# SyncE in written order in the projections, with later stores of the features and recall's loads one place ahead

## The chip, the cores and the metric

The kernel runs on one core of one Trainium2 chip. The metric is the device time of one execution in microseconds (us). TensorE is called PE, VectorE DVE, ScalarE ACT, GpSimd POOL, and SyncE SP; SP issues every DMA of this kernel.

## The reference

```python
x = A_x                                                    # [1, 2048, 576]
g = sigmoid((x * gate_w).sum(-1, keepdims=True))
# A: 32 heads of 18, N = 4 segments of L = 512 tokens, with a memory M, z that runs over the segments
phi = lambda t: where(t > 0, t + 1.0, exp(t))
for s in range(4):
    qs, ks, vs = q[:, :, s], k[:, :, s], v[:, :, s]
    a_dot = softmax(qs @ ks.T * 18 ** -0.5 + causal mask) @ vs
    a_mem = (phi(qs) @ M) / (phi(qs) @ z + 1e-6)
    outs.append(sigmoid(beta) * a_mem + (1 - sigmoid(beta)) * a_dot)
    M, z = M + phi(ks).T @ vs, z + phi(ks).sum()
a = concat(outs) @ wo
b = (gelu(x @ w_gate) * (x @ w_up)) @ w_down               # 576 -> 4608 -> 576
out = g * a + (1 - g) * b
```

## The kernel before, in words

All large products are made in pairs of float16 words (high and low), three matmuls for one. The kernel has two parts. The first, up to about 241 us, makes the projections q, k, v of the four segments, the memory and the recall from it. The second is a loop of 72 steps, with the feed-forward part and the attention interleaved, and then the output projection.

The first part goes over the segments s = 0 to 3. A segment s has *rows* (for s > 0): four groups q of 128 tokens, in which `vrows` makes v in two halves (q, 0) and (q, 1), `key_rows` transposes phi(k) of the segment before, and `memorize` adds to the memory's product. Then come its *columns*: nine chains j = 0 to 8 of 14 matmuls each (`project`), 128 columns of q and k at a time. What a chain leaves in PSUM is read in the next column (`put_columns`): ACT takes the high word, an exponential for phi follows on ACT, DVE makes phi and the low word (`rest`, `words`), POOL adds the exponential, and two DMAs store the words to `qk`. `rest` is put off into a list (`later`) that `finish_later` works off a little later in the same column.

For s >= 1 phi(q) of a segment is kept as float32 and split later by `split_phi` (ACT high, POOL low, two stores to the DRAM tile `phq`). In segment s + 1, `load_phi(s, g)` loads the features of eight heads (two DMAs, 256 KB each, into the single buffer `phg`), `recall(s, g)` multiplies them with the memory (16 small matmuls into two banks, "st" or "dn"), and `put_recall` divides on DVE and stores to `om`. The four groups g = 0 to 3 follow each other. In the last segment's case (s = 3) they run in the first steps of the loop.

The memory's own chain runs in the columns of the next segment: `keep_memory` at j = 1, `memory_squares` at j = 2, `memory_scales` at j = 4 (a sum on PE, a root on DVE, six small operations on POOL), `memory_pairs` at j = 6 (two ACT copies, a POOL subtraction, two stores to `md`, two loads into `mpair`, which recall multiplies with).

`load_x16` loads a segment of x (three DMAs, 1280 KB) and `load_sums` two segments once more (two DMAs of 1024 KB each). `load_g` loads a block of w_gate and w_up (640 KB); ACT squares it, and the sums of the squares (`scales(0)`, in the rows of s = 3 at q = 1) stand in PE's order.

PE, ACT, DVE and POOL run in the order in which the code is written (`manual_schedule(engines=ORDERED)`). SP is not in that set before the change: the scheduler chooses the order of the DMAs. The PSUM tags are "dn" and "st" with two banks each, and "pv", "V", "G", "U" with one.

Of the kernel before, what the change touches and what calls it, by code (L numbers as in the profile page):

```python
# [18 lines left out]
P = 128  # L19
# [26 lines left out]
def kernel(ctx: ExitStack, tc: tile.TileContext, xs, wqk, wv, wo, wgu, wd, beta, out):  # L46
# [8 lines left out]
    def bank(tag, bufs=1, dt=F32):  # L55
        return ps.tile([P, 512 if dt == F32 else 1024], dt, name=tag, tag=tag, bufs=bufs)
# [20 lines left out]
    def root(out, inv, src):  # L77

        dve.tensor_scalar(out.bitcast(I32), src.bitcast(I32), 1, EXP, OP.logical_shift_right, OP.bitwise_and)
        dve.tensor_scalar(inv.bitcast(I32), out.bitcast(I32), EXP, None, OP.bitwise_xor)  # L80
# [12 lines left out]
    def sums(st, o=None):  # L93

        o = (spare() if o is None else o)[:, : st.shape[1]]
        pe.matmul(o, onesb, st.bitcast(BF16)[:, 1::2], start=True, stop=True)
        return o
# [461 lines left out]
    if True:  # L559
# [15 lines left out]
        xt = [mp.tile([P, 15, L], F16, name="xt0", bufs=1)]  # L575
        kept.update(words=flat(acc), xt=xt)
        pa = first.enter_context(tc.tile_pool(name="early", bufs=2, reuse_waits="tile"))
        W, phi, vst, kr, mem, phis, phg, ghs = {}, {}, {}, {}, {}, [], {}, {}
        QG = ((0,), (1,), (2,), (3,), (4, 5), (6, 7), (8,))
        VG = ((0,), (1,), (2,), (3,), (4,))  # L580
        VB = (slice(0, NH), slice(NH, D + 2))
# [78 lines left out]
        def split_phi(until):  # L660
            while phis and phis[0][:2] <= until:
                s, j, f = phis.pop(0)
                m = min(P, D - j * P)
                st = pp.tile([P, 2, L], F16, name="stage", bufs=5)
                act.activation(st[:m, 0], f[:m], AF.Copy)
                pool.tensor_tensor(st[:m, 1], f[:m], st[:m, 0], OP.subtract)
                r = phq[s - 1][j * P : j * P + m]
                sp.dma_start(r[:, :2], st[:m])
                sp.dma_start(r[:, 2], st[:m, 0])

        def load_phi(s, g):
            r = phq[s - 1].rearrange("f a t -> (f a) t")
# [5 lines left out]

        def put_columns(s, j, pr):
            hf, c = divmod(s, 2)  # L680
            st = pp.tile([P, 2, L], F16, name="stage", bufs=5)
            unit = unq if j < 4 else 2.0**-14
            i = 2 if j < 4 else 0
# [144 lines left out]
                act.activation(m16[:, :, 2, c], mc[:, :, c], AF.Square, accum_out=q[:, i : i + 1])  # L828
            return q

        def memory_scales(s, q):
            o = sums(q, bank("dn", 2))
            v = pp.tile([P, 2, 2], F32, name="mv", bufs=1)
            z = pp.tile([P, 2], F32, name="mz", bufs=1)
            dve.tensor_scalar(z, o, 1e-30, None, OP.max)
            root(v[:, 0], v[:, 1], z)
            u = pp.tile([P, 2], F32, name="mu", bufs=1)
            pool.tensor_scalar(u, v[:, 1], 2.0**-50, None, OP.mult)
            g, eps = ghs[s + 1] = pp.tile([P, H], F32, name="ghs", bufs=2), pp.tile([P, 1], F32, name="eps", bufs=2)
            for i, c in enumerate((slice(0, DH), slice(DH, MC))):  # L840
                pool.tensor_scalar(mt[:, :, c], mc[:, :, c], u[:, i : i + 1], None, OP.mult)
            pool.tensor_scalar(g, gh[:, 0], u[:, 1:2], v[:, 0, 0:1], OP.mult, OP.mult)
            pool.tensor_scalar(g, g, 2.0**49, None, OP.mult)
            pool.tensor_scalar(eps, u[:, 1:2], kmc[:, s + 1, 1:2], 1e-6, OP.mult, OP.mult)

        def memory_pairs():
            act.activation(m16[:, :, 0], mt, AF.Copy)
            act.activation(m16[:, :, 1], m16[:, :, 0], AF.Copy)
            pool.tensor_tensor(m16[:, :, 2], mt, m16[:, :, 0], OP.subtract)
            sp.dma_start(md[: 4 * MT].rearrange("(j p) a c -> p j a c", p=MT), m16[:MT, :4])  # L850
            sp.dma_start(md[4 * MT :], m16[: D - 4 * MT, 4])
            n = 3 * DH
            r = md.rearrange("(i e f) a c -> e (f a) i c", e=2, f=DH)
            for e in range(2):
                sp.dma_start(mpair[64 * e : 64 * e + n, :, e * MC : (e + 1) * MC], r[e])
# [19 lines left out]
            dve.tensor_scalar(gate[:, 1, gs], gate[:, 0, gs], -1.0, 1.0, OP.mult, OP.add)  # L875

        FIRST = (0,)
        with tc.manual_schedule(engines=ORDERED):
            pool.memset(onesb, 1.0)

            start = bank("G")
# [214 lines left out]
            for s in range(4):  # L1096
                p = s - 1
                if s:
                    for q in range(4):
# [15 lines left out]
                        pv = vrows(s, q, 1)  # L1115
                        put_rows(s, q, 1, *pv)
                        if p >= 1:
                            if q < 2:
                                split_phi((p, 2 if q == 0 else 4))
                            else:  # L1120
                                recall(p, q - 2)
                            if q:
                                load_phi(p, q - 1)
                        if q:
                            memorize(p, q - 1)
                    finish_later()
# [1 line left out]
                for j in range(9):  # L1128
# [39 lines left out]
                    if s and j == 2:  # L1168
                        square = memory_squares()
                    if s and j == 4:  # L1170
                        memory_scales(p, square)
                    if s > 1 and j in (3, 5):
                        recall(p, (j + 1) // 2, "dn")
                        if j == 3:
                            load_phi(p, 3)
                    if s and j == 6:
                        memory_pairs()
                    if s == 3 and j == 8:
                        load_phi(3, 0)
            put_columns(*done)  # L1180
            finish_later()
            split_phi((3, 4))
            ahead[0] = first_product(0)
            finish_later()

# [801 lines left out]
```

## Time and profile before

| what | value |
|---|---|
| median of 3 runs | 1591.38 us (1590.36 to 1592.06) |
| profiled execution | 1592.69 us, its span 1591.0 us |
| PE busy | 1550.5 us, 97% of the span |
| DVE, ACT, POOL busy | 1265.6, 1217.6, 1161.4 us |
| PE idle in 100.79 to 241.40 us | 32.1 us of 140.6 |
| granted clock of PE over the span | 0.99 |

The span is the time from the first to the last instruction of the profiled execution; the device time holds 1.7 us more. Lines as L758 are lines of the kernel before. A bracket behind a row of the timeline says how long the engine was idle before it and what ended that. The last row but one counts PE's idle time from the rows of s = 2 to the end of the first part.

### The profile page before, as it was taken

What the parts mean: (1) busy time and instruction counts of PE and PEld (TensorE: products, weight loads), DVE (VectorE), ACT (ScalarE), POOL (GpSimd) and SP (SyncE); (2) the same over time, 40 slices, a digit from 0 to 9 for tenths busy, and PEclk for the clock granted to TensorE, in tenths of its full rate; (3) what the DMA queues carried; (4) which work ended last, traced back from release to release, by engine and by line L of the source; (5) the groups of instructions that cost most, each with busy time, mean ns of one, the idle gap of its engine ahead of it and who ended that gap; (6) DMA issues with size and microseconds to landing.
All of it is one profiled execution on the core that took longest, in us unless ns stands there. A gap on an engine that the chain in (4) does not pass through costs nothing.

```text
span 1591.0 us, 33969 instructions
## 1 busy us (share of the span) xinstructions
PE 1550.5 (97%) x12271; PEld 944.8 (59%) x12271; DVE 1265.6 (80%) x3249; ACT 1217.6 (77%) x2092; POOL 1161.4 (73%) x1260
## 2 busy tenths in 40 slices
PE   9988689999999999999999999999999999999999
PEld 5644444556666665656666556656566666656577
DVE  7867577688888888888888888888888888888665
ACT  7575363588888878888888888888888888887421
POOL 4284485687868687787868696777878686877597
PEclk9999799999999999999999999999999999999999
DMA  6655757246566675656575766567575766755546
GB/s 242 231 170 150 206 169 186 61 111 143 132 149 139 125 146 123 128 125 145 126 156 131 144 141 134 134 121 149 117 151 132 154 136 131 150 117 101 116 83 174
DMA packets 513156, 225.83 MB, mean 142 GB/s; under 512 B 435768, under 2 KB 491804, under 8 KB 512476
## 3 DMA queue, kind: packets, MB, share of 16 engines
q1 hardware_dynamic: 512988, 223.67, 61.2%
q8 instruction: 96, 1.57, 0.4%
q14 instruction: 72, 0.59, 0.1%
HBM read 97.47 MB, written 37.52 MB: 85 GB/s over the span
## 4 chain that ended last, share of the span: by engine, by line
PE 83%; POOL 7%; DVE 3%; ACT 3%; DMA 2%; issue 1%; SPq 0%; POOLq 0%; ACTq 0%; DVEq 0%
PE dn L1337 25%; PE U L535 17%; PE G L535 11%; PE V L535 6%; PE V L1457 5%; PE pv L1290 4%; PE U L1383 2%; PE V L1388 1%; PE G L1388 1%; PE st L1252 1%; PE st L414 1%; PE dn L421 1%; PE V L1383 1%; PE G L1383 1%; PE dn L1252 1%
## 5 line engine op out<-in xcount | busy, mean ns | idle before, releaser
L535 PEld LDWEIGHTS <-pairg 128*128 128x128 f16 x2592 | 247.9, 98 | 263.6 <-issue 17.6
L1273 POOL TENSOR_TENSOR pl<-pb,ph 128x896 f16<-128x896 f32 (+1 forms) x128 | 185.7, 1472 | 211.3 <-ACT ph L1272 211.3
L1337 PE MATMUL dn<-paird,hhr 128*128 128x288 f16 x2115 | 328.7, 286 | 0.1
L1271 ACT ACTIVATE pb<-pb,mb,esc 128x512 f32<-128x512 f32 (+3 forms) x512 | 304.9, 642 | 5.2
L1345 DVE SCALAR_TENSOR_TENSOR acc<-dn,ev,acc 128x288 f32<-128x288 f32 x533 | 262.6, 513 | 39.3 <-PE dn L1337 33.3
L1337 PEld LDWEIGHTS <-hhr 128*128 128x128 f16 x2160 | 207.0, 98 | 78.6 <-issue 11.8
L535 PE MATMUL G<-x,pairg 128*128 128x512 f16 x864 | 210.4, 380 | 5.5 <-DVE stage L703 4.5
L535 PE MATMUL U<-xt,pairg 128*128 128x512 f16 x864 | 209.9, 379 | 0.0
L1337 PE MATMUL dn<-paird,hhd 128*128 128x288 f16 x1275 | 209.8, 286 | 0.0
L1273 POOL TENSOR_TENSOR pb<-pb,ph 128x896 f16<-128x896 f32 (+1 forms) x128 | 179.4, 1402 | 33.3 <-ACT ph L1272 27.7
L1272 ACT ACTIVATE ph<-pb 128x896 f16<-128x896 f32 (+1 forms) x256 | 188.6, 737 | 9.7
L347 POOL TENSOR_TENSOR pairg<-raw,pairg 128x384 f16<-128x384 f32 (+2 forms) x144 | 157.5, 1115 | 20.2 <-ACT pairg L343 20.2
L1255 DVE CUSTOM_DVE_ANT_0 pb<-st,mask 128x512 f32<-128x512 f32 (+1 forms) x256 | 157.2, 614 | 0.0
L1337 PEld LDWEIGHTS <-hhd 128*128 128x128 f16 x1296 | 123.9, 98 | 50.4 <-issue 6.5
L1255 DVE CUSTOM_DVE_ANT_0 pb<-dn,mask 128x256 f32<-128x256 f32 (+1 forms) x192 | 67.2, 375 | 64.2 <-PE dn L1252 62.5
L1457 PE MATMUL V<-xt,nest 128*128 128x256 f16 x714 | 105.5, 272 | 0.0
L535 PE MATMUL V<-x,pairg 128*128 128x512 f16 x426 | 105.1, 383 | 0.1
L535 PE MATMUL U<-x,pairg 128*128 128x512 f16 x432 | 105.0, 379 | 0.2 <-DVE gl L1653 0.2
L1378 ACT ACTIVATE gl<-gl,sc 128x512 f32<-128x512 f32 x110 | 75.8, 715 | 34.0 <-DVE gl L1653 23.0
L1375 POOL TENSOR_TENSOR hhr<-gl,hhr 128x512 f16<-128x512 f32 x64 | 78.9, 1239 | 14.6 <-ACT hhr L1367 14.5
L1290 PEld LDWEIGHTS <-pt 128*128 128x128 f16 x2560 | 80.8, 96 | 13.1 <-issue 8.4
L343 ACT ACTIVATE pairg<-raw 128x384 f16<-128x384 f32 (+2 forms) x144 | 77.8, 587 | 10.1 <-DVE raw L309 6.1
(371 smaller groups left out, 3197.7 us busy)
## 6 DMA issues: line engine op xcount, KB each, us to landing
qkt<-qk SPq DMA_DIRECT2D x256, 108.0 KB
raw<-in_wgu_dram SPq DMA_DIRECT2D x36, 640.0 KB
rawd<-in_wd_dram SPq DMA_DIRECT2D x36, 288.0 KB
qk<-stage SPq DMA_DIRECT2D x32, 256.0 KB
phg<-phq SPq DMA_DIRECT2D x24, 256.0 KB
qk<-stage SPq DMA_DIRECT2D x40, 128.0 KB
vp<-vstage SPq DMA_DIRECT2D x16, 296.0 KB
vt<-vp SPq DMA_DIRECT2D x16, 296.0 KB
```

Source lines behind the costliest of these rows:

```text
L343: act.activation(spot(f, *p, 0), raw_g[f][:, p[0] : p[1]], AF.Copy)
L347: pool.tensor_tensor(spot(f, *p, 1), raw_g[f][:, p[0] : p[1]], spot(f, *p, 0), OP.subtract)
L535: pe.matmul(o, w[:, i, (a + k) * P : (a + k + 1) * P], x[:, b + k], start=start and k == 0 and i == 0 and b == h, stop=k == 1 and i == 1, ...
L1255: dve.tensor_tensor_reduce(scored(a, qi), out[qi], mask[:, L - (qi + 1) * P :], 1.0, -3e38, OP.add, OP.max, mx[a][:, qi : qi + 1])
L1271: act.activation(r, r, AF.Exp, bias=b[:, qi : qi + 1], scale=esc[:, 0, c : c + 1])
L1272: act.activation(h[:, cols], p, AF.Copy)
L1273: pool.tensor_tensor(low[:, cols], p, h[:, cols], OP.subtract)
L1290: pe.matmul(ov, pr[:, 10 * i + COL[qi] // P + kb], v[:, 4 * e + kb, c0 : c0 + VC], start=kb == 0 and i == 0, stop=kb == qi and i == 1)
L1337: pe.matmul(o[:, :NH], hh[:, a, q * P : (q + 1) * P], w[:, b, n * NH : (n + 1) * NH], start=i == 0, stop=i == 5)
L1345: dve.scalar_tensor_tensor(av, o[:, :NH], ev, av, OP.mult, OP.add)
L1375: pool.tensor_tensor(hh[:, 1], t, hh[:, 0], OP.subtract)
L1457: pe.matmul(o, w[:, (7 * c + i) * P : (7 * c + i + 1) * P], x[d], start=start and n == 0, stop=n == 2, skip_group_check=True)
```

## The change

SP joins the engines that keep the written order, in the first part only. `split_phi` no longer issues its two stores but keeps them in a list; `store_phi` issues them at the next place (the next `put_columns`, or the next group of rows). `recall(p, 0)` goes from the rows' q = 2 to q = 3, recall 1 from q = 3 to behind column 1; recalls 2 and 3 stay behind columns 3 and 5. Each load of recall in the columns stands one column ahead of its recall, behind columns 0, 2 and 4. The sum of `memory_scales` becomes `memory_root`, in the bank "pv" and at j = 4; the rest of it follows at j = 5; `memory_pairs` is cut into `memory_high` (j = 6), `memory_low` (j = 7) and `load_pairs` (j = 8).

```diff
         def split_phi(until):
 ...
-                r = phq[s - 1][j * P : j * P + m]
-                sp.dma_start(r[:, :2], st[:m])
-                sp.dma_start(r[:, 2], st[:m, 0])
+                phi_out.append((phq[s - 1][j * P : j * P + m], st[:m]))
+
+        def store_phi():
+            while phi_out:
+                r, st = phi_out.pop(0)
+                sp.dma_start(r[:, :2], st)
+                sp.dma_start(r[:, 2], st[:, 0])
 
         def put_columns(s, j, pr):
             hf, c = divmod(s, 2)
+            store_phi()
 ...
-        def memory_scales(s, q):
-            o = sums(q, bank("dn", 2))
+        def memory_root(q):
+            o = sums(q, bank("pv"))
 ...
             root(v[:, 0], v[:, 1], z)
+            return v
+
+        def memory_scales(s, v):
 ...
-        def memory_pairs():
+        def memory_high():
             act.activation(m16[:, :, 0], mt, AF.Copy)
             act.activation(m16[:, :, 1], m16[:, :, 0], AF.Copy)
+
+        def memory_low():
             pool.tensor_tensor(m16[:, :, 2], mt, m16[:, :, 0], OP.subtract)
 ...
+        def load_pairs():
 ...
-        with tc.manual_schedule(engines=ORDERED):
+        with tc.manual_schedule(engines=ORDERED | {mybir.EngineType.SP}):
 ...
                         if p >= 1:
+                            if q:
+                                store_phi()
                             if q < 2:
                                 split_phi((p, 2 if q == 0 else 4))
-                            else:
-                                recall(p, q - 2)
-                            if q:
-                                load_phi(p, q - 1)
+                            if q == 2:
+                                load_phi(p, 0)
+                            if q == 3:
+                                recall(p, 0)
 ...
                     if s and j == 4:
-                        memory_scales(p, square)
-                    if s > 1 and j in (3, 5):
-                        recall(p, (j + 1) // 2, "dn")
-                        if j == 3:
-                            load_phi(p, 3)
+                        mv = memory_root(square)
+                    if s and j == 5:
+                        memory_scales(p, mv)
+                    if s > 1 and j < 6:
+                        if j % 2:
+                            recall(p, (j + 1) // 2, "dn")
+                        else:
+                            load_phi(p, j // 2 + 1)
                     if s and j == 6:
-                        memory_pairs()
+                        memory_high()
+                    if s and j == 7:
+                        memory_low()
+                    if s and j == 8:
+                        load_pairs()
 ...
             split_phi((3, 4))
+            store_phi()
```

Three places show how SP's order moves. The first is SP in the columns of s = 2, around the load of recall 3 (`phg_1829` before, `phg_1890` after). `stage_1794` and `stage_1844` hold the words of columns 2 and 3 in their order of before and after, and `mo` is what a put_recall leaves. Before:

```order
L709 DMA qk_74<-stage_1724 128x512
L709 DMA qk_74<-stage_1760 128x512
L708 DMA qk_74<-stage_1724 128x2x512
L708 DMA qk_74<-stage_1760 128x2x512
L709 DMA qk_74<-stage_1794 128x512
L677 DMA phg_1829<-phq0_66 64x4x512 x2
L708 DMA qk_74<-stage_1794 128x2x512
L709 DMA qk_74<-stage_1847 128x512
```

After:

```order
L681 DMA phg_1776<-phq0_66 64x4x512 x2
L438 DMA acc_110<-in_xs_dram 128x2048 x2
L713 DMA qk_74<-stage_1794 128x2x512
L714 DMA qk_74<-stage_1794 128x512
L782 DMA om_72<-mo_1870 128x4x144
L713 DMA qk_74<-stage_1844 128x2x512
L714 DMA qk_74<-stage_1844 128x512
L681 DMA phg_1890<-phq0_66 64x4x512 x2
```

The load of recall 3 stood behind one store of column 2, and now stands behind all stores of columns 2 and 3 and behind the store of recall 2's result; the two loads of `load_sums(1)` (L438) stand here too, where before they were issued in segment 0.

The second place is SP at the start of these columns, with the load of recall 1 (`phg_1671`) and of recall 2 (`phg_1776`), after the change:

```order
L150 DMA raw_1663<-in_xs_dram 128x1024
L150 DMA raw_1665<-in_xs_dram 128x1024
L150 DMA raw_1667<-in_xs_dram 128x512
L681 DMA phg_1671<-phq0_66 64x4x512 x2
L713 DMA qk_74<-stage_1693 128x2x512
L714 DMA qk_74<-stage_1693 128x512
L782 DMA om_72<-mo_1760 128x4x144
L713 DMA qk_74<-stage_1747 128x2x512
L714 DMA qk_74<-stage_1747 128x512
L681 DMA phg_1776<-phq0_66 64x4x512 x2
```

The three pieces of x for s = 3, which the scheduler had issued during columns and rows before, now stand right ahead of the load of recall 1, and the load of recall 2 stands behind the stores of columns 0 and 1 and of recall 1's result.

The third place is SP at the end of the columns of s = 2, with the first three loads of w_gate and w_up (L243). Before:

```order
L243 DMA raw_2049<-in_wgu_dram 128x1280
L777 DMA om_72<-mo_1979 128x4x144
L708 DMA qk_74<-stage_1969 128x2x512
L850 DMA md_69<-m16_103 126x4x57
L851 DMA md_69<-m16_103 72x57
L709 DMA qk_74<-stage_2014 128x512
L708 DMA qk_74<-stage_2014 128x2x512
L243 DMA raw_2051<-in_wgu_dram 128x1280
L855 DMA mpair_104<-md_69 54x16x19 x2
L243 DMA raw_2053<-in_wgu_dram 128x1280
```

After:

```order
L713 DMA qk_74<-stage_2009 128x2x512
L714 DMA qk_74<-stage_2009 128x512
L860 DMA md_69<-m16_103 126x4x57
L861 DMA md_69<-m16_103 72x57
L243 DMA raw_2047<-in_wgu_dram 128x1280
L243 DMA raw_2049<-in_wgu_dram 128x1280
L243 DMA raw_2051<-in_wgu_dram 128x1280
L713 DMA qk_74<-stage_2040 128x2x512
L714 DMA qk_74<-stage_2040 128x512
L867 DMA mpair_104<-md_69 54x16x19 x2
```

The three loads were apart, the first ahead of the stores to `md` and the third behind the loads of `mpair`; now they follow each other behind the stores to `md`.

More of the change, by code (lines that the diff above doesn't have):

```diff
@@ L577 @@
         pa = first.enter_context(tc.tile_pool(name="early", bufs=2, reuse_waits="tile"))
-        W, phi, vst, kr, mem, phis, phg, ghs = {}, {}, {}, {}, {}, [], {}, {}
+        W, phi, vst, kr, mem, phis, phi_out, phg, ghs = {}, {}, {}, {}, {}, [], [], {}, {}
         QG = ((0,), (1,), (2,), (3,), (4, 5), (6, 7), (8,))
```

## The prediction

> **What bounds the kernel now.** I read the page first: TensorE is busy for 97% of the span. Cutting the span into the stages of the code shows where the rest lies. The columns are the stretch and its length, then busy time (and count) of PE, weight load, DVE, ACT and POOL, the granted clock, the DMA share and GB/s.
>
> ```profile
> 0.00:100.79 100.79, 97.80 (x578) 58.07 (x579) 75.40 (x174) 68.85 (x132) 47.99 (x84) 1.00 0.63 215
> 100.79:131.75 30.96, 21.57 (x214) 17.71 (x213) 19.55 (x41) 16.04 (x32) 19.91 (x17) 0.89 0.69 197
> 131.75:164.14 32.39, 29.25 (x177) 14.04 (x175) 27.15 (x62) 23.89 (x43) 19.98 (x26) 1.00 0.51 145
> 164.14:202.01 37.87, 25.53 (x216) 20.19 (x215) 20.20 (x49) 13.33 (x32) 13.88 (x17) 0.77 0.67 193
> 202.01:241.40 39.39, 32.18 (x182) 14.93 (x180) 29.35 (x58) 26.87 (x54) 31.88 (x37) 0.96 0.63 188
> 241.40:1591.00 1349.60, 1344.19 (x10911) 819.82 (x10910) 1093.96 (x2868) 1068.65 (x1803) 1027.72 (x1083) 1.00 0.62 132
> ```
>
> The four middle stretches are the rows of s = 2, the columns of s = 2, the rows of s = 3 and the columns of s = 3. They hold 32 of the 40 us that PE is idle, and the change touches nothing after them but a few loads. What PE waited for up to 420 us:
>
> ```profile
> PE st L758 <- DMA vp<-vstage: 7.7, 1, 7.7
> PE dn L96 <- ACT nest L91: 7.6, 1, 7.6
> PE dn L96 <- DVE mo L774: 5.8, 2, 3.1
> PE G L535 <- DVE stage L703: 4.5, 1, 4.5
> PE st L758 <- DMA phg<-phq: 4.2, 2, 4.0
> PE dn L423 <- DVE x L223: 1.6, 1, 1.6
> ```
>
> Two of these are recall waiting for its features (L758; the first names another store, but phg had just been issued beside it), and the 5.8 are the sums of the memory's squares (L96) waiting for the bank that put_recall reads (mo). The 7.6 are the squares of w_gate. Where they stand (start, duration, operation, idle before in brackets):
>
> ```profile
> 123.20 0.69 PE L758 MATMUL st<-mpair,phg 128*128 128x38 f16 x16 [7.74 <-DMA vp<-vstage]
> 129.81 0.55 PE L758 MATMUL st<-mpair,phg 128*128 128x38 f16 x16
> 131.75 3.19 PE L414 MATMUL dn<-x,wp 128*128 128x512 f16 x14
> 135.63 6.21 PE L414 MATMUL st<-x,wp 128*128 128x512 f16 x28
> 144.69 0.56 PE L758 MATMUL dn<-mpair,phg 128*128 128x38 f16 x16
> 148.11 0.38 PE L178 MATMUL V<-pairg,onesb 128*128 128x512 bf16 x1
> 151.63 0.16 PE L96 MATMUL dn<-msq,onesb 128*128 128x2 bf16 x1 [3.14 <-DVE mo L774]
> 154.68 0.56 PE L758 MATMUL dn<-mpair,phg 128*128 128x38 f16 x16
> 192.13 0.67 PE L758 MATMUL st<-mpair,phg 128*128 128x38 f16 x16 [3.98 <-DMA phg<-phq]
> 221.22 0.16 PE L96 MATMUL dn<-msq,onesb 128*128 128x2 bf16 x1 [2.68 <-DVE mo L774]
> 221.24 4.87 PE L414 MATMUL st<-x,wp 128*128 128x512 f16 x14
> 241.40 1.90 PE L535 MATMUL G<-x,pairg 128*128 128x512 f16 x6 [4.53 <-DVE stage L703]
> ```
>
> **Rows of s = 2.** Recall 0 moves from q = 2 to q = 3. Between the two places stand a memorize, two vrows and a key_rows, 129.81 - 123.89 = 5.9 us in the trace, partly at half clock; I take 5.2 at full clock. Both halves of its load now stand behind the stores of the last features; before, only the second half did:
>
> ```profile
> 119.54 0.62 SPq L677 DMA_DIRECT2D phg<-phq  x1
> 161.64 0.34 SPq L243 DMA_DIRECT2D raw<-in_wgu_dram  x1
> 163.14 0.69 SPq L850 DMA_DIRECT2D md<-m  x1
> 166.23 1.52 SPq L243 DMA_DIRECT2D raw<-in_wgu_dram  x1
> ```
>
> So the first half goes out at about 119.5 and the second at 120.1. From issue of a second half to the recall that reads it the trace has 3.7 us (119.54 to 123.20) and, in the chain of waits:
>
> ```profile
> 188.09 3.90 DMA phg<-phq
> 255.66 4.29 DMA phg<-phq
> ```
>
> I take 3.9, with 3.7 and 4.3 as ends. Recall 0 then starts at 124.1 where recall 1 started at 129.81: **-5.7**. PE is ready at 123.20 - 7.74 + 5.2 = 120.7, so a wait of 3.4 stays. That the stores of phi are issued one place behind their split costs nothing by itself: the split on POOL is what they waited for before, and a stage tile (five of them) is not wanted again for four places. If that cover were gone, ACT's next split would wait some 2 us.
>
> **Columns of s = 2.** Three recalls stand here instead of two, after chains 1, 3 and 5, and each load waits in SP's written order. Four DVE rows price it:
>
> ```profile
> 140.35 0.74 DVE L703 SCALAR_TENSOR_TENSOR stage<-dn,unq,stage 128x512 f16<-128x512 f32 x1
> 148.53 0.69 DVE L179 TENSOR_REDUCE x<-V 128x1 f32<-128x512 f32 x1 [0.93 <-PE V L178]
> 151.03 0.82 DVE L774 TENSOR_TENSOR mo<-dn,rden 128x288 f32<-128x288 f32 x2
> 152.43 0.74 DVE L703 SCALAR_TENSOR_TENSOR stage<-U,unq,stage 128x512 f16<-128x512 f32 x1
> ```
>
> Recall 1 needs both dn banks, and chain 0 sits in one of them until its words are read, at 141.1. Chain 1 ends at about 135.63 + 6.21/2 = 138.7. So PE waits 2.4, plus 0.4 for the recall itself. Its load, behind the three pieces of load_x16(3) (1280 KB, newly at this place), should just make it.
>
> The load of recall 2 stands behind om of recall 1 and the two stores of column 1. From the end of recall 1: put_recall 1.8 (148.53 + 1.5 to 151.85), column 1 on DVE 1.4, two issues 0.9, the first half's issue 0.6, landing 3.9, in all 8.6; PE has two chains, 6.1. Wait 2.5.
>
> The load of recall 3 stands behind om of recall 2 and the stores of column 3, which DVE gives at 153.2, because scale_x (L179) and put_recall come first. Then 0.9 + 0.6 + 3.9 brings 158.6, where the trace has 154.68 with its 3.14 wait. The sums in pv save that wait, yet recall 3 is still 3.9 later: PE reaches it at 148.1 + 0.3 + 3.05 = 151.5 and waits 7.1 there. Sum of the stage: 2.8 + 2.5 + 3.9 = **+9.2**. Ends: each landing at 3.7 or 4.3, so 8.8 to 10.0; nothing below, since the DVE rows ahead stay.
>
> The two loads of load_sums(1) (2 MB) come here too, behind the load of recall 2. At the 241 GB/s of a row below they need some 8.7 us and are through before the load of recall 3 goes out. load_sums(0) and load_x16(2) move from 26-60 us to about 55 and 73: SP is free, PE's 97.8 of 100.79 busy hides them, and their readers come after 80. If not, squares of x wait, up to 3 us.
>
> **Rows of s = 3.** Recall 0 has 5.1 us more work ahead of it from 188.1 on, and its load lands at 192.0: **-4.0**, ends -4.0 and -3.6. The squares of w_gate need the first two of three loads:
>
> ```profile
> 168.01 0.74 ACT L597 ACTIVATE krow<-raw 128x640 bf16<-128x640 f32 x1 [1.42 <-DMA raw<-in_wgu_dram]
> 175.40 0.74 ACT L597 ACTIVATE krow<-raw 128x640 bf16<-128x640 f32 x1 [6.57 <-DMA raw<-in_wgu_dram]
> ```
>
> and the ten us around them, in the columns of the first table:
>
> ```profile
> 160.00:170.00 10.00, 10.00 (x68) 6.63 (x67) 7.47 (x17) 6.84 (x12) 9.05 (x8) 1.00 0.94 241
> ```
>
> Before, they left at 161.64 and 166.23 and were there at 168.0 (6.4 us) and 175.4. Now all three leave in one run behind the md stores. Those wait for POOL's subtract and came 7.9 us after recall 3 (163.14 - 155.24). I keep that; two md issues of 0.7 (the first row has 0.69) put the loads at about 9.3. The first lands 6.4 later and the second 2.8 behind it (655 kB at 241 GB/s): 18.5 after recall 3. The last chain ends 3 x 3.05 + 1.5 of half clock = 10.6 after it, so the data come 7.9 behind the stage's end, where it was 175.4 - 164.14 = 11.3. That is 3.4 less; I take **-3.0**, between 0 (the subtract comes later, its step being one column later) and -4.
>
> **Columns of s = 3.** The same waits of 2.4 and more stand here, but PE does not set this stage's end: the 4.53 at 241.40 waits for a chain of POOL, ACT and DVE, with POOL busy 31.88 of 39.39. That chain starts with memory_scales, now one column later, and with DVE's column 3, which moves by put_recall 1 (1.8) and by the wait for the load of recall 2. I put **+2.6**; bounds 0 (the chain absorbs it) and +5 (by the same counting PE waits 2.4, 4 and 2.6 ahead of its three recalls, less the 4.53 that was idle).
>
> **The rest.** POOL's chain for the memory gives way to phi of column 4 in s = 1:
>
> ```profile
> 100.46 0.69 ACT L689 ACTIVATE expm<-st,nal 128x512 f32<-128x512 f32 x1 [2.08 <-POOL phi L698]
> ```
>
> That frees expm sooner, and DVE's L223 with its 1.6: **-1.4**, bounds 0 and -1.6. Half clock: after the wait of 3.98, twelve matmuls of vrows took 3.08, later 1.64.
>
> ```profile
> 194.12 3.08 PE L421 MATMUL dn<-wv,x 128*128 128x288 f16 x12
> 198.34 1.64 PE L421 MATMUL dn<-wv,x 128*128 128x290 f16 x12
> ```
>
> With what stands around them this is some 3 us that go with the wait; the wait of 7 in the columns brings about 1.5 back. Net **-1.5**, bounds -4 and +3.
>
> At nothing I cost the later loads of mpair (two columns later; the recall that reads them is a row stage away, or for s = 3 in the step loop, and if they came late it would wait 1 to 2 us) and the six small POOL operations of memory_scales, which only change places with one phi.
>
> The Trainium skill ("TensorE: Matmul & The Clock Gate", section HAM oscillation) has the PE array fall to half clock after idle gaps of more than about 3.4 us. The row at 151.63 agrees (3.14, clock 1.00); the row at 221.22 does not: 2.68 us, then a chain of 4.87 instead of 3.19. By the rule the new waits of 2.4 and 2.5 are free, as I have them; by that row they could add up to 1.7 each, +3.4.
>
> Sum: -1.4 - 5.7 + 9.2 - 4.0 - 3.0 + 2.6 - 1.5 = **-3.8**. The profiled execution took 1592.69 (span 1591.0 and 1.7 around it); less 3.8 it is 1588.9. It stands 1.3 above the median 1591.38, so I predict a median of **1587.6**.
>
> **Rivals.** (1) The moved loads collide, and it is slower. x16(3) and load_sums(1), 3.3 MB, now lie among the loads of recall 1 to 3. The second w_gate load took 175.4 - 166.23 = 9.2 us in such a crowd, against 3.9. If two loads land 5.3 later, +10.6 gives +6.8, 1598. It decides from +7 on, that is if both are late by more than 3.5. For it: that load's own row, and the 0.94 of DMA share around it. Against it: a DMA share of 0.51 over the columns. (2) The waits cancel: w_gate's wait does not shrink (+3.0) and the clock gains nothing (+1.5): +0.7, 1592. For it: md still gates those loads. (3) Loads are hidden: SP takes stores without delay and recalls find features ready. Then -9.2 in the rows, -2.7 in the columns, -7 in the rows of s = 3, -2 and -1.4, -4 of clock: -26, 1565. Against it: 3.9 us of landing are longer than one chain of 3.1, even with no store ahead.
>
> **How the numbers follow.** Forecast 0.42 (its own range 1583 to 1591), collision 0.25, cancelling 0.25, hidden 0.08. Within 0.2% (3.2 us, about what a measurement of this kernel can tell from no change) lie four fifths of the cancelling case and a quarter of the forecast, whose centre is just beyond that bound; the cancelling case's fifth goes to faster. So faster 0.31 + 0.08 + 0.05 = 0.44, same 0.20 + 0.11 = 0.31, slower 0.25. The range 1577 to 1598 leaves out the hidden case and a tail of the collision.
>
> **What would show it.** Right: no wait of recall in the rows of s = 3; one of about 3.5 in those of s = 2; in the columns of s = 2, waits ahead of the recalls after chains 1, 3 and 5 of 2.4, 2.5 and 7, the first on DVE, the others on phg; no wait on mo ahead of L96; the wait on the squares at 4 to 5; the start of the step loop near 238 instead of 241.4. Wrong: phg loads that leave before the column's stores, or waits of recall above 9.

## The result, and the profile after

The changed kernel took 1602.78 us (median of 4 runs, 1602.29 to 1603.3); the kernel before, run beside it, took 1591.72. The ratio is 1.0071 (95% interval 1.0053 to 1.0088): 11 us slower, where 3.8 less was forecast. The profiled execution took 1603.3 with a span of 1601.5, where it was 1592.69 and 1591.0; the working below goes by the spans (+10.5).

The same stages in the trace after, cut at the same places of the program (columns as in the first table of the prediction):

```profile
0.00:100.71 100.71, 97.47 (x578) 57.21 (x579) 75.73 (x174) 68.06 (x131) 47.14 (x82) 1.00 0.56 192
100.71:129.10 28.39, 21.28 (x198) 17.62 (x197) 21.16 (x41) 16.97 (x34) 21.52 (x19) 0.92 0.52 157
129.10:178.77 49.67, 36.12 (x193) 15.97 (x191) 32.14 (x64) 24.04 (x43) 19.75 (x27) 0.81 0.62 189
178.77:205.86 27.09, 21.84 (x200) 17.02 (x199) 18.61 (x42) 13.28 (x32) 14.83 (x18) 0.94 0.72 220
205.86:251.38 45.52, 33.06 (x198) 15.45 (x196) 29.63 (x62) 27.12 (x54) 29.69 (x35) 0.92 0.60 179
251.38:1601.50 1350.12, 1344.23 (x10911) 819.59 (x10910) 1093.02 (x2868) 1068.44 (x1803) 1028.27 (x1083) 1.00 0.61 132
```

Set against the table of before, with idle time as length less PE's busy time:

| stage | forecast | measured length | of it idle | of it PE busy |
|---|---|---|---|---|
| up to the rows of s = 2 | 0 | -0.1 | +0.2 | -0.3 |
| rows of s = 2 | -1.4 - 5.7 | -2.6 | -2.3 | -0.3 |
| columns of s = 2 | +9.2 | +17.3 | +10.4 | +6.9 |
| rows of s = 3 | -4.0 - 3.0 | -10.8 | -7.1 | -3.7 |
| columns of s = 3 | +2.6 | +6.1 | +5.3 | +0.9 |
| half clock | -1.5 | (in the last column) | | |
| step loop and after | 0 | +0.5 | +0.5 | 0.0 |
| sum | -3.8 | +10.5 | +7.0 | +3.5 |

A recall is 0.4 us of busy time, and one moved from each rows stage to the columns behind it. The rest of the last column is the same work at another granted clock: lower in the columns of s = 2 (0.81, where it was 1.00), higher in the rows of s = 3 (0.94, where it was 0.77). What PE waited for, up to 430 us (wait, times, longest):

```profile
PE dn L763 <- issue: 10.4, 3, 5.1
PE dn L763 <- DMA phg<-phq: 7.9, 2, 7.6
...
PE dn L96 <- ACT nest L91: 3.1, 1, 3.1
PE dn L423 <- DVE x L223: 2.3, 1, 2.3
```

Recall is L763 now. The lines "issue" (the profile shows no releaser) and "DMA phg" are its loads in the columns, 18.3 us together: these are the five recalls that the profile lists as waiting for phg. The waits on mo ahead of L96 are gone, and the squares of w_gate cost 3.1 instead of 7.6. Where the waits stand on PE (start, duration, idle before in brackets):

```profile
125.79 0.67 PE L763 MATMUL st<-mpair,phg 128*128 128x38 f16 x16 [4.71 <-DMA vp<-vstage]
...
129.10 4.24 PE L414 MATMUL dn<-x,wp 128*128 128x512 f16 x14
...
139.53 0.35 PE L763 MATMUL dn<-mpair,phg 128*128 128x38 f16 x8 [1.71 <-DVE stage L708]
...
149.89 0.67 PE L763 MATMUL dn<-mpair,phg 128*128 128x38 f16 x16 [3.96 <-issue]
150.40 5.50 PE L414 MATMUL G<-x,wp 128*128 128x512 f16 x14
...
166.81 0.67 PE L763 MATMUL dn<-mpair,phg 128*128 128x38 f16 x16 [7.64 <-DMA phg<-phq]
167.30 5.59 PE L414 MATMUL st<-x,wp 128*128 128x512 f16 x14
...
187.83 0.17 PE L96 MATMUL dn<-stat,onesb 128*128 128x10 bf16 x1 [3.08 <-ACT nest L91]
...
203.92 0.55 PE L763 MATMUL st<-mpair,phg 128*128 128x38 f16 x16 [1.20 <-DMA vp<-vstage]
...
226.14 0.67 PE L763 MATMUL dn<-mpair,phg 128*128 128x38 f16 x16 [5.06 <-issue]
226.64 4.94 PE L414 MATMUL G<-x,wp 128*128 128x512 f16 x14
...
251.38 2.72 PE L535 MATMUL G<-x,pairg 128*128 128x512 f16 x6 [4.46 <-DVE stage L708]
```

Every wait of the forecast is there, in its place; one of 1.20 stands ahead of recall 0 of s = 3, where none was forecast. Behind three of the waits (149.89, 166.81, 226.14) a chain of 14 matmuls takes 5.50, 5.59 and 4.94 instead of 3.18. SP's queue shows why the loads of recall 2 and 3 come late (start and length of the issue):

```profile
143.84 0.37 SPq L713 DMA_DIRECT2D qk<-stage  x1
...
144.89 1.24 SPq L681 DMA_DIRECT2D phg<-phq  x2
...
159.50 0.37 SPq L782 DMA_DIRECT2D om<-mo  x1
160.86 0.37 SPq L713 DMA_DIRECT2D qk<-stage  x1
...
161.83 1.24 SPq L681 DMA_DIRECT2D phg<-phq  x2
```

The load of recall 2 (144.89) follows the stores of column 1 (143.84). The load of recall 3 (161.83) stands behind om (159.50) and column 3 (160.86), and DVE gives these late, since it first waits for PE. Its rows in the same stretch:

```profile
156.16 0.69 DVE L179 TENSOR_REDUCE x<-V 128x1 f32<-128x512 f32 x1 [8.36 <-PE pv L96]
...
158.66 0.82 DVE L779 TENSOR_TENSOR mo<-dn,rden 128x288 f32<-128x288 f32 x2
```

DVE stood 8.36 us until the sums of x's squares (L178; the row names L96, which runs right behind it) came out of PE behind the slow chain of 150.40; only then could it do scale_x, put_recall 2 and column 3. That order makes the wait of 7.64: from the end of the sums (156.12) it takes 5.7 us until the load goes out and 5.0 more until recall 3 starts, while PE is ready for recall 3 after one chain (155.98). The slow chain of 150.40 delays both sides alike; it costs its own 2.3 us and does not lengthen the wait. In e5 (below) that chain ran in 3.18, and recall 3 still started 7.7 us after the end of the chain ahead of it.

### The profile page after: what moved, and what is told of

The parts are those of the page before. It is cut to its first block, busy times and chain, and to the rows that moved or that the text cites. A ratio compares the mean times of both kernels' runs of the same rounds, so it can differ in the third digit from the quotient of the medians.

```text
span 1601.5 us, 33934 instructions
## 1 busy us (share of the span) xinstructions
PE 1554.0 (97%) x12271; PEld 942.9 (59%) x12271; DVE 1270.3 (79%) x3249; ACT 1217.9 (76%) x2092; POOL 1161.2 (73%) x1260
## 4 chain that ended last, share of the span: by engine, by line
PE 83%; POOL 6%; DVE 3%; DMA 3%; ACT 3%; issue 1%; SPq 1%; POOLq 0%; DVEq 0%; ACTq 0%
PE dn L1359 25%; PE U L535 17%; PE G L535 11%; PE V L535 6%; PE V L1479 5%; PE pv L1312 4%; PE U L1405 2%; PE V L1410 1%; PE G L1410 1%; PE st L1274 1%; PE st L414 1%; DMA phg<-phq 1%; PE V L1405 1%; PE G L1405 1%; PE dn L1274 1%
## 5 line engine op out<-in xcount | busy, mean ns | idle before, releaser
L414 PEld LDWEIGHTS <-wp 128*128 128x128 f16 x504 | 49.8, 101 | 63.8 <-issue 10.8
```

## The experiments

Each ratio is to the kernel before, run beside it (1591.4 to 1591.9 us). "Start of the loop" is the first product of the step loop on PE: 241.40 before, 251.38 after.

### Whose doing: SyncE's order, or the rest

**e2: the kernel before, with SyncE in written order and nothing else.**

```diff
-        with tc.manual_schedule(engines=ORDERED):
+        with tc.manual_schedule(engines=ORDERED | {mybir.EngineType.SP}):
```

> The kernel before, and of the whole change only SyncE in written order. There the loads of recall 2 and 3 stand in the written order right behind the recall that frees the tile. Theory Q: the written order by itself does no harm where the loads are written ahead of the stores; no wait of recall above 4 us in the columns, time 1586 to 1595, my value 1591. Rival W (any written order holds SyncE back at stores whose data are not there yet, and everything behind them): 1598 or more.

1604.51 us, ratio 1.0083 (1.0069 to 1.0096): rival W. The columns kept their waits as theory Q had it (33.8 and 39.4 us long, before 32.4 and 39.4), but the rows of s = 2 took 2.2 more and the stretch from the start of the loop on took 1357.6 instead of 1349.6. Of these 8.0, 4.8 are the first recall, which waits 5.24 instead of 0.43 for a load that SP issued behind stores of features and of columns, and 3.1 are more busy time of PE. SP's queue:

```profile
246.21 2.74 SPq L668 DMA_DIRECT2D phq<-stage  x1
...
251.94 1.28 SPq L677 DMA_DIRECT2D phg<-phq  x2
```

and that recall on PE:

```profile
256.82 0.67 PE L758 MATMUL st<-mpair,phg 128*128 128x38 f16 x16 [5.24 <-DMA phg<-phq]
```

The store of features held SP for 2.74, and the load left 6.5 us after the start of the loop (245.41); in the trace of before it left at 243.21, 1.8 after it.

**e3: the changed kernel without SyncE in written order** (that one line is as it was before).

> The changed kernel without SyncE in written order: the scheduler orders its queue again, the rest of the change stays. There one half of each load stands one to three stores earlier in the queue than in the changed kernel. Theory Q: the waits ahead of recall 2 and 3 shrink by the stores passed but do not vanish, since the load of recall 2 is still not the first thing behind recall 1; 1586 to 1597, my value 1592. Rival R (three recalls in the columns with one tile for the features are too many, whatever SyncE's order): 1600 or more.

1588.81 us, ratio 0.9982 (0.9973 to 0.9991), 14 us below the changed kernel and 2.8 below the kernel before. So the rest of the change is a small gain, and SyncE's order turns it into a loss. The loop starts at 236.05. Of the recalls in the columns, recall 1 still waits for DVE's words (2.1) and recall 2 of s = 3 for its load (3.6); those of s = 2 wait for no load, three though they are: rival R falls.

**e1: the changed kernel, each load directly behind the recall that frees its tile.**

```diff
                             if q == 3:
                                 recall(p, 0)
+                                load_phi(p, 1)
...
                         if j % 2:
                             recall(p, (j + 1) // 2, "dn")
-                        else:
-                            load_phi(p, j // 2 + 1)
+                            if j < 5:
+                                load_phi(p, (j + 3) // 2)
```

> The changed kernel with one move: each recall's features are asked for directly behind the recall that frees the tile, ahead of the stores that SyncE took first (load of recall 1 behind recall 0, of 2 behind 1, of 3 behind 2). Theory Q (the place in SyncE's queue): the load of recall 2 leaves at the end of recall 1, about 5 us earlier, and lands before PE has done its two chains (6.1 us); the wait of 4.0 ahead of recall 2 and the one of 7.6 ahead of recall 3 in the columns of s = 2 fall below 1 us each, the chains after them run in 3.2 us instead of 5.5, and likewise in the columns of s = 3. Time 1577 to 1590, my value 1583. Theory C (the loads are slow because x16(3) and load_sums(1) move beside them): the loads leave earlier and still land late, waits of 3 us or more stay, time above 1597.

1590.9 us, ratio 0.9998 (0.9989 to 1.0007): 12 us of the loss are given back by moving three loads per s past the column's stores, SyncE still in written order. The columns of s = 2 on PE:

```profile
138.05 0.35 PE L763 MATMUL dn<-mpair,phg 128*128 128x38 f16 x8 [2.11 <-DVE stage L708]
138.25 4.87 PE L414 MATMUL st<-x,wp 128*128 128x512 f16 x14
...
145.97 0.56 PE L763 MATMUL dn<-mpair,phg 128*128 128x38 f16 x16
...
155.84 0.67 PE L763 MATMUL dn<-mpair,phg 128*128 128x38 f16 x16 [3.02 <-DMA phg<-phq]
156.34 4.54 PE L414 MATMUL st<-x,wp 128*128 128x512 f16 x14
...
178.89 0.17 PE L96 MATMUL dn<-stat,onesb 128*128 128x10 bf16 x1 [6.16 <-ACT nest L91]
...
237.55 2.72 PE L535 MATMUL G<-x,pairg 128*128 128x512 f16 x6 [6.47 <-DVE stage L708]
```

Recall 2 waits no more. Three things stand between this and the 1583 that I expected: recall 3 still waits 3.02, and two chains of s = 2 are slow (4.87 and 4.54 instead of 3.18); the squares of w_gate wait 6.16 again instead of 3.1 (their loads stand where they stood, but PE comes earlier), and at 237.55 the loop waits 6.47 for DVE, where it was 4.46. Waits above 1 us stayed, so theory Q holds for the place of the loads and not for the time.

### The rival of colliding transfers

**e4: the changed kernel, load_sums(1) beside load_sums(0), load_x16(3) at the start of the rows of s = 2.**

> The changed kernel with the two large loads taken out of the columns of s = 2: load_sums(1) is issued beside load_sums(0) in the rows of s = 1, load_x16(3) at the start of the rows of s = 2. Theory Q: nothing is gained, since the loads of recall 2 and 3 stand behind the same stores; waits of 3.5 to 4.5 and 7 to 8 stay, 1600 to 1604. Theory C (collision): from issue of the second half to the recall falls from 4.4 to 3.7 us and below, the waits shrink by 1 us or more each, time at or below 1598.

1602.15 us, ratio 1.0069 (1.0055 to 1.0082), no difference. The recalls still waited (2.3 and 7.5 in the columns of s = 2, 5.6 in those of s = 3): theory Q. One wait did shrink as theory C had it, that of recall 2 from 3.96 to 2.26, but the chain behind it stayed slow (4.87) and the one behind recall 1 became so (4.87 instead of 3.18); the loop starts at 250.01, 1.4 earlier. Theory C falls as the main cause of this result. **e13** made the same two moves in the kernel with three moves (e9, below), where the loads leave in time:

> The kernel with the three moves, and load_sums(1) beside load_sums(0) in the rows of s = 1, load_x16(3) at the start of the rows of s = 2. Where the loads of the features leave in time, recall 3 of s = 2 still waits 2.8 us, for a load issued at 149.5 and there at 156.0, right behind the 2 MB of load_sums(1). Theory C (collision): without these 2 MB beside it the load lands 1 to 2 us sooner, the wait of 2.8 falls below 1, the chain behind it runs in 3.2 instead of 4.9; time 1580.5 to 1583, my value 1582. Rival: the load is late because it stands behind column 2's stores (issued at 149.5, when recall 2 had ended at 147.0), and lands in 4 us anyway: 1583.5 to 1585.5.

1585.16 us, ratio 0.9958 (0.9944 to 0.9971), against 1584.29 for e9: nothing in the time, a miss. Yet a small collision is there: the load of recall 3 leaves at the same point (149.79, in e9 149.50), and the recall waits 1.02 instead of 2.76, with a chain of 3.18 behind it instead of 4.87. The columns of s = 2 fell from 38.6 to 34.1 us; 1.7 of that is the chain behind recall 1 (3.18 instead of 4.87), whose wait is 2.11 in both. The gain is given back elsewhere: the columns of s = 2 start 1.3 later, the rows of s = 3 take 2.3 more (28.7 instead of 26.4, with a new wait of 1.98 for x's low words, L223), and the first recall of the loop waits 2.11 instead of 0.57. This is read from one profile of each.

### The half clock

**e5: the changed kernel, with matmuls that nobody reads ahead of four recalls.**

```diff
...
+            for _ in range(fill):
+                pe.matmul(o[0][:, :P], onesb, onesb, start=True, stop=True)
...
-                                recall(p, 0)
+                                recall(p, 0, fill=34 if s == 2 else 0)
...
```

> The changed kernel with work that nobody reads put on PE ahead of four recalls that wait: small matmuls of ones (128 x 128, some 0.11 us each) into the recall's own bank, 34 ahead of recall 0 of s = 2, 30 and 60 ahead of recalls 2 and 3 of s = 2, 37 ahead of recall 2 of s = 3. They end a little before the features land. Theory K (the half clock behind a wait is a cost of its own, set off by PE standing still): the chains behind these recalls fall from 5.5, 5.6, 4.9 and 4.2 us to 3.2, the granted clock of the columns of s = 2 rises from 0.81 to 0.95 or more, the waits themselves do not go, and the time is 1592 to 1598, my value 1595.5. Rival: the clock follows something else (the transfers, or the time of the program); chains stay at 4.9 to 5.6 and the time at 1601 to 1604.

1600.23 us, ratio 1.0053 (1.004 to 1.0065). On PE:

```profile
121.28 2.06 PE L761 MATMUL st<-onesb 128*128 128x128 bf16 x34
125.70 0.56 PE L765 MATMUL st<-mpair,phg 128*128 128x38 f16 x16 [2.35 <-issue]
...
127.64 3.19 PE L414 MATMUL dn<-x,wp 128*128 128x512 f16 x14
...
148.64 0.55 PE L765 MATMUL dn<-mpair,phg 128*128 128x38 f16 x16 [0.86 <-DMA phg<-phq]
149.04 3.18 PE L414 MATMUL G<-x,wp 128*128 128x512 f16 x14
...
152.31 3.18 PE L414 MATMUL st<-x,wp 128*128 128x512 f16 x14
155.49 3.52 PE L761 MATMUL dn<-onesb 128*128 128x128 bf16 x60
163.16 0.67 PE L765 MATMUL dn<-mpair,phg 128*128 128x38 f16 x16 [4.14 <-DMA phg<-phq]
163.66 5.59 PE L414 MATMUL st<-x,wp 128*128 128x512 f16 x14
```

The fillers took half of what I had planned (34 in 2.06 us), so they left waits of 2.35, 0.86 and 4.14. Behind the first two the chains ran in 3.19 and 3.18 instead of 4.24 and 5.50; behind the third it stayed at 5.59, and behind a rest of 2.78 in the columns of s = 3 at 4.87. The transfers around them stayed, so where PE's idle time was filled the slow chain went (theory K, at two of four places): it is a cost beside the wait. The wait itself did not depend on it: recall 3 started 7.7 us after the chain ahead of it (155.49 to 163.16), as in the changed kernel. PE came earlier to recall 1, which then waited 3.41, with a chain of 4.48 behind it. The loop started at 247.35, 4.0 earlier; the median is 2.5 lower, between the ranges of the theory and of the rival, and its interval just overlaps that of the changed kernel.

### Single terms of the forecast

**e6: the changed kernel, split of the last features ahead of the differences of x on POOL (rows of s = 2).**

```diff
             def behind_rows(s, q):
-                if s == 2 and q < 3:
+                if s == 2 and q == 2:
                     form_sums(0, q, -1, pool)
...
                                 split_phi((p, 2 if q == 0 else 4))
+                                if s == 2:
+                                    form_sums(0, q, -1, pool)
```

> The changed kernel with one order on POOL turned round in the rows of s = 2: the split of the last features (two short operations each) goes ahead of the differences of x (one operation of 3.1 us) in places q = 0 and 1. Theory: recall 0 of s = 2 waits 4.7 us because its loads stand in SyncE's order behind the stores of a split that POOL does late; the last stores then leave 2 to 3 us earlier, the wait falls to 1 to 2.5, the chain of column 0 returns from 4.2 to 3.2, time 1597 to 1600, my value 1598.5. Rival: the landing of vp and phg sets it, or DVE's L223 (2.3 us) does; 1602 to 1604.

1604.07 us, ratio 1.0082 (1.0068 to 1.0096): a miss. Recall 0 had its features and waited for nothing, but PE waited ahead of it, for DVE, and DVE for ACT, which stood 3.52 and 4.32 us until POOL's differences were there:

```profile
115.79 1.65 PE L421 MATMUL dn<-wv,x 128*128 128x290 f16 x12 [1.28 <-DVE gate L735]
...
123.70 2.16 PE L421 MATMUL dn<-wv,x 128*128 128x290 f16 x12 [2.54 <-DVE gate L735]
...
126.14 0.71 PE L763 MATMUL st<-mpair,phg 128*128 128x38 f16 x16
```

It starts at 126.14 where it started at 125.79. Behind the load stands POOL's work, and the -5.7 of the forecast were not to be had by the load alone.

**e14: e9, with ACT's copy of memory's words one column later.** In the changed kernel this copy (memory_high, L855) stayed in column 6 while POOL's memory_scales went to column 5. On ACT, in the kernel before (L847):

```profile
97.31 0.27 ACT L847 ACTIVATE m<-mt 128x95 f16<-128x95 f32 x1
```

and in the changed kernel:

```profile
100.17 0.28 ACT L855 ACTIVATE m<-mt 128x95 f16<-128x95 f32 x1 [2.84 <-POOL mt L849]
```

> The kernel with the three moves, and ACT's copy of memory's words (memory_high, for s = 1 and 2) one column later, directly ahead of POOL's subtract. Theory: the copy now waits 2.8 us on ACT for POOL's memory_scales, which the change put one column later while the copy stayed where it was; eviction and expm of column 5 behind it are late, and with them DVE's L223, on which PE waits 2.3 us in the rows. Without it that wait falls below 0.8 us; recall 0 starts where its load and POOL let it, so that little of this is left: 1582.5 to 1584.5, my value 1583.5. Rival: L223 waits for ACT's own work and for POOL's phi, as before the change (1.55 there): the wait stays at 1.5 to 2.3, and the stores to md get later by one column, 1584 to 1586.5.

1584.74 us, ratio 0.9954 (0.9942 to 0.9967). The wait of PE for L223 (2.31) is gone, as the theory said, and two of 0.8 stand in its place; recall 0 then waits 4.74, and the columns begin at 128.61 as ever (128.64 in e9); the time is that of e9, just above the theory's range. **e15** had e13's and e14's moves together:

> The kernel with the three moves, with both: the large loads early and ACT's copy one column later. If the two are independent, what each gains adds: 1580 to 1582.5, my value 1581. If the columns of s = 2 then wait for DVE's words of column 0 in the bank of dn (2.1 us ahead of recall 1) and for POOL as before, no more than the better of the two: 1582 to 1584.

1584.26 us, ratio 0.9956 (0.9944 to 0.9969): no more than e9.

**e11: the changed kernel, the stores of the features directly behind their split again.**

> The changed kernel with one part undone: the stores of the features are written directly behind their split again, SyncE still in written order. Theory Q: in the columns and rows of s = 2 and 3 the waits of recall come from the stores of the columns, not from these; nothing changes by more than 1.5 us, 1601.5 to 1604.5. Rival: SyncE stands at these stores until POOL has done the split, and the loads behind it are late (as at the start of the step loop of the kernel before with SyncE in written order, where a recall waited 5.2): 1606 or more.

1607.17 us, ratio 1.0092 (1.0077 to 1.0108), 4.4 above the changed kernel; the intervals overlap, but each of its four runs lies above each of the changed kernel's. The trace has part of the place: the loop starts 2.4 later (253.76), the stores to md leave at 251.67 instead of 248.03, behind stores of features, and a recall of the step loop waits 2.58 instead of 0.86. The time is the rival's: in written order the place of these stores seems to matter.

**e12: the changed kernel, the sums of memory's squares in a bank of dn again.**

> The changed kernel with one part undone: the sums of memory's squares go back to a bank of dn, which put_recall reads. Theory: PE then waits about 3.5 us for put_recall 2 ahead of these sums in the columns of s = 2, but recall 3 has its load no earlier and its wait of 7.6 shrinks by as much; in the columns of s = 3 recall 3's wait is 1.4, so some 1 to 2 us are lost there. 1602.5 to 1605.5, my value 1604. Rival: the waits add, as the bank of pv was forecast to save 3.1 and 2.7: 1607 or more.

1600.51 us, ratio 1.0055 (1.0043 to 1.0068): a miss, for it is not slower, if anything 2.3 faster.

```profile
158.28 0.16 PE L96 MATMUL dn<-msq,onesb 128*128 128x2 bf16 x1 [3.14 <-DVE mo L779]
158.30 6.07 PE L414 MATMUL st<-x,wp 128*128 128x512 f16 x14
165.81 0.56 PE L763 MATMUL dn<-mpair,phg 128*128 128x38 f16 x16 [1.43 <-issue]
```

The wait on mo is back (3.14), and recall 3's wait shrank from 7.64 to 1.43, since its load comes when it comes. The slow chain (6.07) now runs ahead of that load and not behind it.

### What is left, and a kernel that beats both

**e7: e1, with the loads of w_gate ahead of the stores to md** (load_g(0), load_g(1) in column 7, not 8).

> The kernel with the load behind the recall, and beside it the first two loads of w_gate one column earlier, ahead of the stores to md that wait for POOL's subtract. Theory: the wait of 6.2 on w_gate's squares in the rows of s = 3 is these stores' place ahead of the loads; the loads leave 4 to 5 us earlier, the wait falls to 1 to 2.5, time 1585 to 1588, my value 1586.5. Rival: the squares wait for the transfer itself, at 241 GB/s beside others, or what is gained is taken back at the step loop, whose start waits for POOL: 1590 to 1592.

1586.9 us, ratio 0.9969 (0.9958 to 0.9981), as forecast; PE waited no more for the squares.

**e8: e1, with the last column's eviction and memory's words ahead of the pairs of w_gate (s = 3).**

```diff
+                    if s == 3 and j == 8:
+                        finish_later()
+                        put_columns(*done)
+                        finish_later()
                     beside_products(s, j)
...
                         memory_scales(p, mv)
+                        if s == 3:
+                            memory_high()
+                            memory_low()
...
-                    if s and j == 8:
+                    if s and j == (8 if s < 3 else 6):
                         load_pairs()
...
-            put_columns(*done)
             finish_later()
```

> The kernel with the load behind the recall, and two moves at the end of the columns of s = 3: the last column is taken from its bank ahead of the pairs of w_gate on ACT, and memory's words are made directly behind memory_scales, ahead of those pairs on POOL, with their stores and loads two columns earlier. Theory: the step loop starts 6.5 us after PE's last chain because ACT's eviction of that bank stands behind a chain of POOL, and its first recall waits for md and mpair behind the same POOL; the loop then starts at 232 to 234 instead of 237.6 and the recall has no new wait: 1584 to 1588, my value 1586. Rival: the next product needs another thing of POOL's chain, the wait only moves: 1589 to 1592.

1589.26 us, ratio 0.9986 (0.9977 to 0.9995). The loop started at 234.49, 3.1 earlier than in e1, and its first recall waited 2.00 instead of 1.52. The profiled span is 2.5 shorter than that of e1, the median 1.6 lower: a part of the gain that I expected, and the rival's range by time.

**e9: these three together** (e1, e7, e8).

> The changed kernel with three moves together: the load of a recall directly behind the recall that frees the tile, the first two loads of w_gate ahead of the stores to md, and the last column's eviction and memory's words ahead of the pairs of w_gate in the columns of s = 3. If their gains add (4.0 for the second on the first, 1.6 for the third), the time is 1583 to 1586.5, my value 1585. If the step loop's start takes back the second's gain, since it waits for POOL: 1587 to 1590.

1584.29 us, ratio 0.9955 (0.9943 to 0.9968): the gains add, and it is faster than both kernels. **e10** has e8's two moves in e3:

> The changed kernel without SyncE in written order, and with the two moves at the end of the columns of s = 3 (last column's eviction and memory's words ahead of the pairs of w_gate). Without the moves its step loop started at 236.1 after a wait of 6.0 for the last column's eviction. If the moves are worth here what they were worth with SyncE in order, 1586 to 1588, my value 1587; if the start of the loop hangs on POOL's work alone, 1588 to 1590.

1585.68 us, ratio 0.9962 (0.995 to 0.9975). With its loads well placed, SyncE in written order does no worse than the scheduler's order.

## Why the prediction was wrong

**The change itself** was read rightly: the waits came after chains 1, 3 and 5, on DVE's words and on the loads; no wait on mo; the squares waited less. The sum failed on sizes, in two terms above all: the half clock, put at -1.5, came to +3.8, and the rows of s = 2, put at -7.1, came to -2.6. Forecast and measured stand 14.3 apart: the clock is 5.3 of it (busy time over the four stages), the waits in the rows of s = 2 are 4.4 (idle -2.3 for -6.7, which is the forecast -7.1 without the recall's 0.4), those in the columns of s = 3 2.7 (idle +5.3 for +2.6), those in the columns of s = 2 1.6 (idle +10.4 for 8.8, which is the forecast 9.2 less the recall's 0.4); the rest lies outside the four stages.

- **Rows of s = 2, -5.7 and -1.4.** The load left later: its second half went out at 121.5, not 120.1, since the split came 0.7 later and a store ahead of it took 1.22. Recall 0 started at 125.79, not 124.1. And the -1.4 was wrong in sign: the order that should free expm made ACT's copy wait 2.84 for POOL (e14). Moreover the two terms were not independent. The -5.7 set recall 0's start by its load, so what is saved ahead of recall 0 is only waited for there (e14), and without that wait PE stands for POOL's differences (e6).
- **Half clock, -1.5.** The gain of 3 in the rows of s = 3 came (busy -3.7, 0.4 of it the recall); the loss in the columns of s = 2 was 6.5 (busy +6.9 less the recall), where I had 1.5. I set one chain's loss for the wait of 7 and none for those of 2.4 and 2.5. In the columns of s = 2 the chains lost 1.05, 2.3 and 2.4; in those of s = 3 1.8. e5 shows at two of these places that the cost goes when the idle time is filled. I saw the row that spoke for it (2.68, then 4.87) and kept +3.4 out of the sum.
- **Columns of s = 2, +9.2.** Recall 1 waited 1.95 (forecast 2.4), recall 2 3.96 (2.5), recall 3 7.64 (7.1). put_recall 1 took 2.6 from the recall's end and not 1.8; the second half took 4.4 to land and not 3.9. Small each; the mechanism, stores ahead of the load in SP's queue, is shown by e1 and e3.
- **Rows of s = 3, -7.0.** Idle -7.1. Recall 0 kept a wait of 1.20, and the squares waited 3.08, where 4 to 5 was forecast; PE came later.
- **Columns of s = 3, +2.6.** I let the chain of POOL absorb half. It begins with column 4's phi, behind recall 2's wait of 5.06 and the slow chain, and so it moved whole: it starts 27.9 us into the stage (POOL, 233.74) instead of 21.8 (223.85, then with memory_scales), it is as long as before (17.6 us to the start of the loop), and the wait at its end stayed (4.46 for 4.53). Where the waits are gone (e1) the chain does take back what is gained: 6.47.
- **The rivals.** Collision (1598) came nearest in time and was not the main cause (e4). Cancelling (1592) does not fit, since the wait on the squares of w_gate did shrink (7.60 to 3.08). "Loads are hidden" is what e1 and e9 come near to, though at 1590.9 and 1584.3, not 1565: the end chain and DVE's bank keep their waits, and recall 3 of s = 2 still waits 3.02 and 2.76.

The Trainium skill ("TensorE: Matmul & The Clock Gate", section HAM oscillation) has the half clock follow gaps above some 3.4 us. The waits of the changed kernel agree: 1.71 ahead of recall 1 left the next chain at 3.18, while 3.96, 7.64 and 5.06 were followed by slow ones. e1 does not: 2.11 (138.05) was followed by 4.87.

## What to carry to other kernels

A queue put in written order gives every load the lateness of the latest data of any store ahead of it: write a load at the point where its buffer comes free, ahead of the stores whose data are still to be computed. Where PE has chains of 3 us between waits, price a new wait with the slow chain that may stand behind it. The next wait does not grow by that chain where the next load hangs on the same chain as PE's next step. Do not add up gains that lie ahead of the same wait, since the last one to arrive keeps them all. A step moved one place later takes with it whoever reads it and was not moved.

## What was not expected of the hardware

The same wait at the same place is followed by a slow chain in one run and by a fast one in another: 2.11 us ahead of recall 1, then 4.87 in e1 (above) and e9, 3.18 in e8 and in e7, here on PE:

```profile
129.17 4.15 PE L414 MATMUL dn<-x,wp 128*128 128x512 f16 x14
...
139.50 0.35 PE L763 MATMUL dn<-mpair,phg 128*128 128x38 f16 x8 [2.11 <-DVE stage L708]
139.70 3.18 PE L414 MATMUL st<-x,wp 128*128 128x512 f16 x14
```

In e7 the chain before that wait (129.17) had been slow, 4.15, and in e1 it took 3.19. So one wait's length doesn't decide. All ten runs with this wait (2.11 or 2.12) go the same way: where column 0's chain had taken 3.19 to 3.68 (e1, e3, e4, e9, e14) the chain behind the wait took 4.87, and where it had taken 3.84 to 4.38 (e7, e8, e10, e13, e15) 3.18. At recall 1 of s = 3 that order does not hold: with a chain of 3.19 in column 0, a wait of 1.84 was followed by 4.87 in e10 and one of 2.51 by 3.18 in e7. What decides stays open.

Matmuls of ones (128 x 128) took 0.061 us each in the filler (2.06 for 34) and 0.113 at the very start of the kernel (3.38 for 30, the first work of PE in the changed kernel), by which I had planned it:

```profile
1.04 3.38 PE L895 MATMUL G<-onesb 128*128 128x128 bf16 x30 [1.04 <-POOL onesb L891]
```
